# One branch-free stream of 192 slots per expert, with the up projection in unsplit fp32

## The chip, the core and the metric

The kernel runs on one core of a Trainium2 chip. The metric is the device time of one execution in microseconds; a time stands for the median of several executions.

## What is computed

Strided sparse attention (2 batches, 8 heads, 576 tokens, 64 dimensions a head) feeds a dense feed-forward block of 1152 tokens, and that feeds a routed mixture of 8 experts. The change touches the last part only:

```python
logits = x @ w_gate                                   # 1152 tokens, 8 experts
expert_idx = np.argmax(logits, axis=1)
...                                                   # gate_w: softmax probability of the chosen expert
for i in range(N):                                    # first come, first served, capacity 288 an expert
    e = expert_idx[i]
    if counts[e] < capacity:
        disp[e, counts[e]] = x[i]; pos[i] = counts[e]; counts[e] += 1; keep[i] = True
h = np.maximum(np.einsum('ecd,edf->ecf', disp, w1), 0.0)    # 512 -> 1024
y = np.einsum('ecf,efd->ecd', h, w2)                        # 1024 -> 512
out[i] = gate_w[i] * y[expert_idx[i], pos[i]]               # kept tokens, the others are zero
```

All numbers are fp32. Each expert has 2 MB of `w1` and 2 MB of `w2`.

## The kernel before

**Stages.** Attention, then the feed-forward block (`l1`, `l2`, in four groups of 512 hidden columns), with routing work (`r_...` functions) threaded into its last group by `pump`; at the end the experts, one after the other. The order of instructions on each engine is the order in which the code emits them: nothing reorders them, and each engine works through its own queue. DMA loads are issued from SP's queue (weights) and from POOL's (gathers of token rows from `x2d` by `gather`, scatters of results to `out` by `put_out`); an issue that has to wait holds up what stands behind it in that queue.

**Split matmuls.** A value is kept as a high part and a low part in the type fp32r; `mm3` (lines 165 to 168) multiplies in three steps, high by high, high by low and low by high. An fp32r matmul stands in the program as one instruction and in the trace as one weight load and one matmul.

**The expert stage** (from line 1036). Token slots of an expert are three chunks of `ROWS` = 128, 64 and 96. For each expert `e`:

- `prep` (line 922) transposes the gathered rows of chunk 0 and 1 of the next expert (4 matmuls each) and splits them: ACT writes the high part, DVE the low part of `X`.
- `split`/`esplit` (lines 233 to 239) turn each of 8 pieces of 128x1024 raw weights of the next expert into a high part (`whi`, ACT or DVE, line 238) and a low part (`wlo`, DVE or POOL, line 239) and then issue the load of the same piece for the expert after it.
- An expert with at most 128 tokens goes through `narrow`: four `up(i)` of 48 matmuls in all (3 for each of 4 row blocks of `w1`, 256 columns each, tokens as the stationary side), ReLU on ACT, a transpose back (`turn`, line 1083), and `down`, 24 matmuls of 512 columns.
- An expert with more than 128 goes through `wide`: eight `up(i)` of 4 pairs, line 1122 (`whi` against both halves of 192 tokens, 384 columns) and line 1124 (`wlo` against the high half, 192 columns); the two halves of the result are added by ACT and DVE (lines 1127, 1128); ReLU is split again (lines 1136, 1138); `down` is 5 matmuls of 512 columns, three into `y` (tokens 0 to 127) and two into `z` (tokens 128 to 191, both halves stacked).
- Which one is taken is decided on the device. `r_final` writes a flag word, every engine loads it (`get_flags`), and each expert stands under `tc.If` (lines 1226 and 1229; expert 0 under line 1214). Each engine meets these branches in its own queue. A third way, `more`, handles slots beyond 192.

```python
        with tc.If((flags[0] & (3 << 2 * e)) < 1) as small:
            narrow(e, P, y0, fillers(e, False))
        with small.Else():
            with tc.If((flags[0] & (2 << 2 * e)) > 0) as most:
                ...
                wide(e, y0, y1, fillers(e, True), {})
                more(e, y1)
            with most.Else():
                ...
                wide(e, y0, y1, fillers(e, True), {})
        put_out(e, 0, y0)
```

`put_out` (line 1051) scales by the gate and scatters the rows to `out`. For chunk 1 it needs an ACT copy, a DVE add and an ACT scaling. Two scatters in a row wait for each other, since both write `out`.

Of the kernel before, what the change touches and what calls it, by code (L numbers as in the profile page):

```python
# [9 lines left out]
F32 = mybir.dt.float32  # L10
# [8 lines left out]
P = 128  # L19
# [6 lines left out]
N1 = 64  # L26
# [13 lines left out]
W2 = 0  # L40
W3 = 0
LAGW = 3
TT = 3
SPLIT_AT = ((0, 1, 2, 3, 4, 5, 6, 7), (0, 1, 2, 3, 4, 5, 7, 7))
PREP_AT = ((4, 5), (5, 6))
# [3 lines left out]
for _name, _w in (("ident", 128), ("ml", KW), ("ml0", KW), ("ms", 54), ("tri", 128),  # L49
                  ("rev", 8), ("bit", 8), ("tok", 18), ("iota", PW)):  # L50
    _C[_name] = (_off, _w)
    _off += _w
# [4 lines left out]
def constants():  # L57
# [18 lines left out]
    put("bit", np.broadcast_to(4.0 ** np.arange(8), (P, 8)))  # L76
# [12 lines left out]
def tile_kernel(ctx, tc, cap, q, k, v, w_in, w_out, w_gate, w1, w2, consts, out):  # L89
# [125 lines left out]
    SLOTS = ((4, 5, 0, 1), (2, 3, 6, 7))  # L215
    eraw = {}

    def eload(e, h):
        if e >= E:
            return  # L220
        j, r = divmod(h, 2)
        if e == 0 or (e == 1 and h < 4):
            eraw[e, h] = rawp.tile([P, 2, 512], F32, tag="raw", name="raw")
        elif e == 1:
            eraw[e, h] = rawq.tile([P, 2, 512], F32, name=f"raw{h}")
        else:
            eraw[e, h] = eraw[1, h]
        if j < 2:
            src = w1[e][:, 512 * j:512 * j + 512].rearrange("(k p) f -> p k f", p=P)
        else:  # L230
            src = w2[e][512 * (j - 2):512 * (j - 1), :].rearrange("(c p) n -> p c n", p=P)
        nc.sync.dma_start(out=eraw[e, h], in_=src[:, 2 * r:2 * r + 2])

    def esplit(e, h, hi, lo):
        raw = eraw[e, h]
        j, r = divmod(h, 2)
        slot, k = SLOTS[e % 2][j], slice(2 * r, 2 * r + 2)
        (nc.scalar.copy if hi == "A" else nc.vector.tensor_copy)(whi[slot][:, k], raw)  # L238
        (nc.vector if lo == "D" else nc.gpsimd).tensor_sub(wlo[slot][:, k], raw, whi[slot][:, k])  # L239
# [373 lines left out]
    for s in range(2, 6):  # L613
        alloc_w(wpb, s)

# [184 lines left out]
    def r_final():  # L800
# [4 lines left out]
        f = rp.tile([1, 2, E], F32, name="flag", bufs=1)  # L805
        for j in range(2):
# [234 lines left out]
    for i in (6, 7):  # L1041
        alloc_w(wpc, i)
# [225 lines left out]
```

## Time and profile before

| | |
|---|---|
| median of 3 runs | 510.21 us |
| lowest, highest | 506.58 us, 512.13 us |
| span of the profiled execution, first to last instruction | 507.0 us |
| TensorE (PE) busy, share of that span | 87% |
| mean granted TensorE clock | 0.920 |

The span is that of one execution; the device time of an execution also holds what lies around its first and last instruction, which the profile does not show. In the profile PE is TensorE's matmuls, PEld its weight loads, DVE VectorE, ACT ScalarE, POOL GpSimd, SP SyncE. "Issue" as a releaser means that the engine waited for nothing that the profile shows.

### The profile page before, as it was taken

How to read it: one execution, taken by the hardware profiler on the slowest of the kernel's cores; microseconds unless marked ns; L12 is line 12 of the kernel's file. 1: busy time of each engine (PE TensorE's matmuls, PEld its weight loads, DVE VectorE, ACT ScalarE, POOL GpSimd, SP SyncE). 2: the span in 40 equal slices, each digit the busy share in tenths (PEclk: the TensorE clock that was granted, in tenths of full speed). 3: DMA queues.
4: the chain of work that ended last, by engine and by line, in shares of the span. 5: the costliest groups of instructions: out<-in, count | busy, mean ns of one | idle time of the engine just before them, and what ended most of it. 6: DMA issues, size and time to landing. Idle time of an engine off the chain costs nothing.

```text
span 507.0 us, 8500 instructions
## 1 busy us (share of the span) xinstructions
PE 443.6 (87%) x2959; PEld 377.6 (74%) x2959; DVE 345.1 (68%) x782; ACT 235.8 (47%) x587; POOL 198.8 (39%) x180
## 2 busy tenths in 40 slices
PE   8899998999998999999999998798547949498885
PEld 4577677899897899989998788686537748286774
DVE  3569899357788837885445877948684929559571
ACT  4568677245543433444443435355334425244631
POOL 0225433013232311336552154639664426263550
PEclk9969699999998999999999997989796969879989
DMA  7899727023343311344441126735863636535300
GB/s 158 177 233 230 202 85 244 10 53 113 124 126 95 114 41 62 105 125 123 127 146 43 63 75 209 229 127 204 294 224 130 222 116 197 180 113 194 108 25 22
DMA packets 52194, 69.33 MB, mean 137 GB/s; under 512 B 19608, under 2 KB 29080, under 8 KB 52124
## 3 DMA queue, kind: packets, MB, share of 16 engines
q1 hardware_dynamic: 50268, 63.18, 42.1%
q0 software_dynamic: 1856, 5.26, 2.9%
q8 instruction: 38, 0.62, 0.6%
q14 instruction: 32, 0.26, 0.2%
HBM read 61.60 MB, written 7.34 MB: 136 GB/s over the span
## 4 chain that ended last, share of the span: by engine, by line
PE 49%; DVE 23%; issue 13%; ACT 6%; DMA 6%; POOL 1%; POOLq 0%; DVEq 0%; ACTq 0%; another core or an unknown queue 0%
DVE wlo L239 5%; PE acc L166 5%; DVE wsb L194 4%; PE acc L167 4%; DMA out_dram<-y,idx_o 4%; PE h L166 4%; PE h L168 4%; PE acc L168 4%; PE h L167 4%; PE u L1122 4%; DVE g L261 2%; PE acc L406 2%; DVE gl L269 2%; ACT gh L268 2%; PE acc L466 2%
## 5 line engine op out<-in xcount | busy, mean ns | idle before, releaser
L239 POOL TENSOR_TENSOR wlo<-raw,whi 128x1024 fp32r<-128x1024 f32 x36 | 88.9, 2479 | 58.7 <-ACT whi L238 40.0
L203 POOL TENSOR_TENSOR wlo<-w,whi 128x512 fp32r<-128x512 f32 x32 | 44.3, 1385 | 117.6 <-DVE gl L269 79.5
L1122 PE MATMUL u<-X,whi 128*128 128x384 f32 x128 | 49.2, 437 | 24.5 <-issue 24.5
L239 DVE TENSOR_TENSOR wlo<-raw,whi 128x1024 fp32r<-128x1024 f32 x28 | 64.6, 2307 | 5.1 <-ACT whi L238 4.9
L166 PE MATMUL acc<-whi,gh 128*128 128x512 f32 x144 | 59.0, 410 | 2.8 <-DVE x L290 2.8
L166 PE MATMUL h<-xhi,whi 128*128 128x384 f32 x176 | 60.1, 341 | 0.0
L168 PE MATMUL h<-xhi,wlo 128*128 128x384 f32 x176 | 59.5, 338 | 0.0
L167 PE MATMUL h<-xlo,whi 128*128 128x384 f32 x176 | 59.5, 338 | 0.0
L167 PE MATMUL acc<-wlo,gh 128*128 128x512 f32 x144 | 58.1, 403 | 0.0
L168 PE MATMUL acc<-whi,gl 128*128 128x512 f32 x144 | 57.3, 398 | 0.0
L238 ACT CAST whi<-raw 128x1024 fp32r<-128x1024 f32 x50 | 52.4, 1054 | 0.0
L268 ACT CAST gh<-g 128x384 fp32r<-128x384 f32 x48 | 24.6, 513 | 59.1 <-DVE g L261 59.1
L1122 PEld LDWEIGHTS u<-X,whi 128*128 128x128 f32 x128 | 29.9, 234 | 26.6 <-issue 25.8
L261 DVE TENSOR_TENSOR g<-h,g 128x384 f32<-128x384 f32 x44 | 24.3, 553 | 34.8 <-ACT g L260 34.8
L269 DVE TENSOR_TENSOR gl<-g,gh 128x384 fp32r<-128x384 f32 x48 | 28.1, 585 | 25.6 <-ACT gh L268 25.5
L260 ACT ACTIVATE g<-h 128x384 f32<-128x384 f32 x44 | 21.5, 489 | 48.5 <-PE h L168 48.3
L194 DVE SCALAR_TENSOR_TENSOR wsb<-raw,wsb 128x512 uint32<-128x512 uint32 x32 | 39.2, 1226 | 1.0
L421 ACT ACTIVATE pr<-sc,st 128x54 f32<-128x54 f32 (+1 forms) x84 | 28.8, 345 | 19.8 <-DVE st L418 19.8
L1124 PE MATMUL u<-X,wlo 128*128 128x192 f32 x128 | 36.4, 285 | 0.0
L166 PEld LDWEIGHTS h<-xhi,whi 128*128 128x128 f32 x176 | 33.1, 188 | 2.1
L167 PEld LDWEIGHTS h<-xlo,whi 128*128 128x128 f32 x176 | 33.1, 188 | 1.9
L166 PEld LDWEIGHTS acc<-whi,gh 128*128 128x128 f32 x144 | 27.5, 191 | 8.2 <-ACT w L191 3.6
(246 smaller groups left out, 1036.8 us busy)
## 6 DMA issues: line engine op xcount, KB each, us to landing
raw<-in_moe_w_dram SPq DMA_DIRECT2D x64, 512.0 KB
raw<-in_moe_w_in_dram SPq DMA_DIRECT2D x16, 512.0 KB
raw<-in_moe_w_out_dram SPq DMA_DIRECT2D x16, 512.0 KB
out_dram<-zw SPq DMA_DIRECT2D x1, 2304.0 KB
x2d<-x SPq DMA_DIRECT2D x2, 768.0 KB
vl<-in_v_dram SPq DMA_DIRECT2D x4, 288.0 KB
kr<-in_k_dram SPq DMA_DIRECT2D x4, 288.0 KB
qr<-in_q_dram SPq DMA_DIRECT2D x4, 288.0 KB
```

Source lines behind the costliest of these rows:

```text
L166: nc.tensor.matmul(o, lhsT=ah, rhs=bh, start=first, stop=False)
L167: nc.tensor.matmul(o, lhsT=ah, rhs=bl, start=False, stop=False)
L168: nc.tensor.matmul(o, lhsT=al, rhs=bh, start=False, stop=last)
L194: nc.vector.scalar_tensor_tensor(out=u, in0=top, scalar=0x80000000, in1=u, op0=ALU.bitwise_and, op1=ALU.bitwise_or)
L203: nc.gpsimd.tensor_sub(wlo[slot][:, k], t, whi[slot][:, k])
L238: (nc.scalar.copy if hi == "A" else nc.vector.tensor_copy)(whi[slot][:, k], raw)
L239: (nc.vector if lo == "D" else nc.gpsimd).tensor_sub(wlo[slot][:, k], raw, whi[slot][:, k])
L261: nc.vector.tensor_mul(a, h, a)
L268: nc.scalar.copy(gh, a)
L269: nc.vector.tensor_sub(gl, a, gh)
L1122: nc.tensor.matmul(hp[:, 0:2 * NW], lhsT=whi[j][:, kk, o:o + P], rhs=x[:, kk].rearrange("p a n -> p (a n)"), start=kk == 0, stop=False)
L1124: nc.tensor.matmul(hp[:, 0:NW], lhsT=wlo[j][:, kk, o:o + P], rhs=x[:, kk, 0], start=False, stop=kk == KC - 1)
```

## The change

The routing up to the flag stays. In the expert stage:

- `w1` is no longer split: its pieces are loaded straight into whole fp32 tiles `w1b` (three of them, in turn), those of experts 0 and 1 during the feed-forward block. `X` is one fp32 tile.
- Every expert takes 192 slots: `up` is 4 matmuls in plain fp32 of 192 columns each, `relu` reads the result from PSUM and splits it, `down` is that of `wide`.
- The eight experts are one sequence of 64 steps, without a branch; `down` runs 3 steps behind `up`, across the seam between experts.
- `w2` is split as before, 4 pieces an expert, two experts ahead of need in loading, high part on ACT, low part on DVE (expert 0: on POOL, in the feed-forward block).
- Slots beyond 192 are handled under a single `tc.If` at the end, which loads and splits all weights again; its flag is set if any expert has more than 192 tokens.
- `put_out` for chunk 1 takes one ACT and one DVE instruction instead of three, and both result tiles have two buffers.

```diff
+    def w1load(e, j):
+        if e < E:
+            for r in range(2):
+                nc.sync.dma_start(out=w1b[e % 3][:, 2 * r:2 * r + 2, 512 * j:512 * j + 512],
+                                  in_=w1[e][256 * r:256 * r + 256, 512 * j:512 * j + 512]
+                                  .rearrange("(k p) f -> p k f", p=P))
...
+    def split(e, h, ahead=2):
...
+        nc.scalar.copy(whi[slot][:, k], raw)
+        (nc.vector if e else nc.gpsimd).tensor_sub(wlo[slot][:, k], raw, whi[slot][:, k])
+        w2load(e + ahead, h)
...
-        xh, xl = (X[e % 2][:, :, i, o:o + n] for i in range(2))
-        nc.scalar.copy(xh, src)
-        nc.vector.tensor_sub(xl, src, xh)
+        nc.vector.tensor_copy(X[e % 2][:, :, o:o + n], src)
...
-            nc.scalar.copy(y[:n], yp[N1:2 * N1])
-            nc.vector.tensor_add(y[:n], yp[:n], y[:n])
-            nc.scalar.mul(y[:n], y[:n], g)
+            nc.scalar.activation(out=y[:n], in_=yp[N1:2 * N1], func=AF.Copy, scale=g)
+            nc.vector.scalar_tensor_tensor(out=y[:n], in0=yp[:n], scalar=g, in1=y[:n], op0=ALU.mult, op1=ALU.add)
...
-    def narrow(e, n, yp, fill):
...
-    def wide(e, y0, y1, fill, tt, part=(0, 8)):
...
+    def up(e, i, n=NW):
+        hp = psum("u")
+        for kk in range(KC):
+            nc.tensor.matmul(hp[:, 0:n], lhsT=w1b[e % 3][:, kk, P * i:P * i + P], rhs=X[e % 2][:, kk, 0:n],
+                             start=kk == 0, stop=kk == KC - 1)
+        return hp
+
+    def relu(hp, parts, n=NW):
+        t = ep.tile([P, 2 * NW], F32R, tag="ht", name="ht", bufs=LAG + 1)
+        nc.scalar.activation(out=t[:, 0:n], in_=hp[:, 0:n], func=AF.Relu)
+        for o, c, m in parts:
+            nc.vector.scalar_tensor_tensor(out=t[:, o:o + m], in0=hp[:, c:c + m], scalar=0.0, in1=t[:, c:c + m],
+                                           op0=ALU.max, op1=ALU.subtract)
+        return t
...
     for e in range(E):
...
+        fill(e, 3 if e == 0 else 0, (gather, e + 2, 0))
+        fill(e, 4 if e == 0 else 1, (gather, e + 2, 1))
+        for h in range(4):
+            fill(e, SPLIT_AT[h], (split, e + 1, h))
+        fill(e, 5, (prep, e + 1, 0))
+        fill(e, 6, (prep, e + 1, 1))
+        for j in range(2):
+            fill(e, 3 + 4 * j, (w1load, e + 3, j))
+    fill(3, 0, (get_flags,))
...
+    for s in range(8 * E + LAG):
+        e, i = divmod(s, 8)
+        if s < 8 * E:
+            hp = up(e, i)
+        d, c = divmod(s - LAG, 8)
+        if s >= LAG:
+            if c == 0:
+                ys[d] = psum("y"), psum("z")
+            down(d, c, ht.pop((d, c)), *ys[d])
+        for f, *args in fills.pop((e, i), []):
+            f(*args)
+        if s < 8 * E:
+            ht[e, i] = relu(hp, PARTS)
+        if s >= LAG and c == 7:
+            y0, y1 = ys.pop(d)
+            put_out(d, 1, y1)
+            put_out(d, 0, y0)
...
+    with tc.If(flags[0] > 0):
...
```

**Where the instructions stand, PE.** On PE, at the seam between expert 0 and expert 1. Before, expert 0's last `down` ends at two branches, behind which expert 1's `narrow` begins (`h` is its PSUM tile, `X_3345` the tokens):

```order
L1149 MATMUL z<-whi_97,kept_3699 128x512
L1150 MATMUL z<-wlo_98,kept_3699 64x512
L1150 MATMUL z<-wlo_98,ht 64x512
L1152 MATMUL z<-whi_97,ht 128x512
L166 MATMUL y<-whi_97,ht 128x512
L167 MATMUL y<-wlo_98,ht 128x512
L168 MATMUL y<-whi_97,ht 128x512
L1214 UNCONDITIONAL_BRANCH
L1226 REGISTER_ALU
L1226 COMPARE_AND_BRANCH
L166 MATMUL h<-whi_1515,X_3345 128x256
L167 MATMUL h<-wlo_1516,X_3345 128x256
```

Now, the last `up` of expert 0 (`X_3334`, `w1b_1519`), a `down` of expert 0, and the first `up` of expert 1 (`X_3335`, `w1b_1520`):

```order
L1055 MATMUL u<-X_3334,w1b_1519 128x192 x4
L161 MATMUL y<-whi_97,ht 128x512
L162 MATMUL y<-wlo_98,ht 128x512
L163 MATMUL y<-whi_97,ht 128x512
L1074 MATMUL z<-whi_97,ht 128x512
L1075 MATMUL z<-wlo_98,ht 64x512
L1055 MATMUL u<-X_3335,w1b_1520 128x192 x4
```

The branches are gone from PE's queue, the ups of expert 1 stand before the last three downs of expert 0, and an `up` is 4 instructions where `wide` had 8.

**DVE.** On DVE, two steps of a wide expert before: the sum of the two halves (`hs`), the low part of a weight piece, the two low parts of the ReLU, the next sum, and a high part of a weight piece:

```order
L1128 TENSOR_TENSOR hs<-u,hs 128x192
L239 TENSOR_TENSOR wlo_1522<-raw,whi_1521 128x1024
L1138 SCALAR_TENSOR_TENSOR ht<-hs,ht 128x64
L1138 SCALAR_TENSOR_TENSOR ht<-hs,ht 128x128
L1128 TENSOR_TENSOR hs<-u,hs 128x192
L238 CAST whi_95<-raw_3684 128x1024
```

Now, two steps in the stream, the second with the copy of the next expert's tokens:

```order
L236 TENSOR_TENSOR wlo_98<-raw_3675,whi_97 128x1024
L1063 SCALAR_TENSOR_TENSOR ht<-u,ht 128x64
L1063 SCALAR_TENSOR_TENSOR ht<-u,ht 128x128
L932 COPY X_3334<-m 128x4x128
L1063 SCALAR_TENSOR_TENSOR ht<-u,ht 128x64
L1063 SCALAR_TENSOR_TENSOR ht<-u,ht 128x128
```

The sums and the high parts of weights are gone from DVE; the low parts of the ReLU now read PSUM (`u`) directly.

## Rows read from the trace of the kernel before

**Rows 1.** Page: granted TensorE clock in 40 slices, tenths of full speed.
```profile
PEclk9969699999998999999999997989796969879989
```

**Rows 2.** Stretches: length, busy us PE, PEld, DVE, ACT, POOL; clock, DMA share, GB/s.
```profile
0.00:307.30 307.30, 295.12 (x2136) 249.62 (x2137) 211.65 (x591) 150.15 (x419) 98.88 (x122) 0.95 0.43 119
307.30:501.30 194.00, 148.46 (x830) 127.93 (x826) 133.43 (x192) 84.97 (x168) 98.90 (x58) 0.87 0.51 168
336.70:352.20 15.50, 13.44 (x89) 11.58 (x87) 10.14 (x11) 11.19 (x20) 11.04 (x7) 1.00 0.47 167
352.20:383.10 30.90, 15.26 (x89) 13.30 (x89) 21.85 (x15) 10.21 (x17) 19.70 (x10) 0.81 0.79 268
...
501.30:507.00 5.70, 0.00 (x1) 0.00 (x0) 0.00 (x0) 0.69 (x1) 0.99 (x1) 0.80 0.11 45
```

**Rows 3.** PE's waits in the expert stage: us in total, times, longest us.
```profile
PE u L1122 <- issue: 24.5, 4, 9.4
PE m L1083 <- DVE wlo L239: 7.0, 2, 5.9
PE z L1152 <- DVE ht L1138: 7.0, 3, 2.4
PE m L931 <- DVE tt L1086: 3.5, 2, 3.3
PE h L166 <- issue: 2.1, 1, 2.1
PE m L804 <- DVE idx L778: 1.4, 1, 1.4
```

**Rows 4.** Line 1229, TensorE's sequencer: duration ns min/median/max, first and last start us.
```profile
L1229 PEldq COMPARE_BRANCH  x3: 4934/5615/6585, 377.9 to 437.9; - x3
```

**Rows 5.** Groups of PE, shapes apart: busy us, mean ns of one, idle before.
```profile
L1122 PE MATMUL u<-X,whi 128*128 128x384 f32 x128 | 49.2, 437 | 24.5 <-issue 24.5
...
L406 PE MATMUL acc<-kt,qs 64*64 64x96 f32 x144 | 9.1, 261 | 1.0 <-ACT qs L379 0.5 <-DVE qs L379 0.5
```

**Rows 6.** Timeline of PE in expert 0: start us, length us.
```profile
315.00 0.36 PE L1122 MATMUL u<-X,whi 128*128 128x384 f32 x1
315.20 0.25 PE L1124 MATMUL u<-X,wlo 128*128 128x192 f32 x1
315.29 0.37 PE L1122 MATMUL u<-X,whi 128*128 128x384 f32 x1
...
315.58 0.42 PE L166 MATMUL y<-whi,ht 128*128 128x512 f32 x1
...
316.76 0.31 PE L786 MATMUL m<-R,mt 128*128 128x24 bf16 x6
```

**Rows 7.** Plain fp32 matmuls: timeline of a run, and ns of one (min/median/max).
```profile
15.88 0.58 PE L406 MATMUL acc<-kt,qs 64*64 64x96 f32 x10
...
L406 PE MATMUL acc<-kt,qs x10: 242/243/243, 15.9 to 16.2; 64*64 64x96 f32 x10
...
296.22 0.83 PE L652 MATMUL h<-wg,xt 128*128 128x24 f32 x6
...
L652 PE MATMUL h<-wg,xt x6: 269/270/270, 296.2 to 296.8; 128*128 128x24 f32 x6
L652 PEld LDWEIGHTS h<-wg,xt x5: 192/192/192, 296.3 to 296.7; 128*128 128x128 f32 x5
```

**Rows 8.** DVE's weight subtraction (line 239) and ReLU remainder (line 1138), ns min/median/max.
```profile
L239 DVE TENSOR_TENSOR wlo<-raw,whi x28: 1207/1636/8244, 314.1 to 490.4; 128x1024 fp32r<-128x1024 f32 x28
...
L1138 DVE SCALAR_TENSOR_TENSOR ht<-hs,ht x58: 208/277/2411, 311.4 to 468.3; 128x64 fp32r<-128x64 f32 x29, 128x128 fp32r<-128x128 f32 x29
```

**Rows 9.** The scatter, line 1063: the last one, and landing times of all.
```profile
502.30 0.99 POOL L1063 DMA_INDIRECT out_dram<-y,idx_o  x1 [11.05 <-ACT y L1062]
...
DMA to landing us min/median/max: 2.2/3.2/6.9
```

**Rows 10.** Busy us and granted clock in a stretch of the attention stage.
```profile
54.20:64.40 10.20, 10.12 (x78) 7.85 (x77) 8.32 (x37) 7.07 (x29) 5.53 (x7) 0.50 0.64 190
```

More of the change, by code (lines that the diff above doesn't have):

```diff
@@ L39 @@
 WHOLE = 6
[L40 to L45, printed above, removed]
+LAG = 3
+SPLIT_AT = (0, 2, 4, 6)
 _C = {}
@@ L911, in tile_kernel @@
     xg2 = eg.tile([P, DM], F32, name="xg2")
-    X = [eg.tile([P, KC, 2, NW], F32R, name=f"X{i}") for i in range(2)]
+    X = [eg.tile([P, KC, NW], F32, name=f"X{i}") for i in range(2)]
     def xg_of(e, ch):
@@ L1166, in fillers @@
-    def fillers(e, wide):
-        steps = [[] for _ in range(9)]
-        for c in range(2):
-            steps[PREP_AT[wide][c]].append((prep, e + 1, c))
-        for h in range(8):
-            steps[SPLIT_AT[wide][h]].append((split, e + 1, h))
-        steps[0].append((gather, e + 2, 0))
-        steps[1].append((gather, e + 2, 1))
-        return filler(steps)
-    def filler(steps):
-        def fill():
-            for f, *args in (steps.pop(0) if steps else []):
-                f(*args)
-        return fill
@@ L1183, in tile_kernel @@
-    for h in range(4, 8):
-        eload(1, h)
+    def up(e, i, n=NW):
[11 more added lines that the diff above has]
+        return t
@@ new lines, in down @@
+    def down(e, i, t, y0, y1):
+        j, c = 2 * (e % 2) + i // 4, i % 4
+        for y in ((y1, y0) if i == 7 else (y0, y1)):
+            if y is y0:
+                mm3(y0, t[:, 0:P], t[:, 2 * P:3 * P], whi[j][:, c], wlo[j][:, c], i == 0, i == 7)
+            else:
+                if i < 7:
+                    nc.tensor.matmul(y1, lhsT=t[:, P:2 * P], rhs=whi[j][:, c], start=i == 0, stop=False)
+                nc.tensor.matmul(y1[:N1], lhsT=t[:, P:NW], rhs=wlo[j][:, c], start=False, stop=False)
+                if i == 7:
+                    nc.tensor.matmul(y1, lhsT=t[:, P:2 * P], rhs=whi[j][:, c], start=False, stop=True)
@@ new lines, in tile_kernel @@
+    assert not fills, fills
+    with tc.If(flags[0] > 0):
+        n = ROWS[2]
+        for e in range(E):
+            gather(e, 2)
+            w1b[e % 3] = w1b[0]
+            for j in range(2):
+                w1load(e, j)
+            for h in range(4):
+                w2raw[e, h] = w2raw[1, h]
+                nc.sync.dma_start(out=w2raw[e, h],
+                                  in_=w2[e][256 * h:256 * h + 256, :].rearrange("(c p) n -> p c n", p=P))
+                split(e, h, E)
+            prep(e, 2)
+            y2 = psum("y")
+            for i in range(8):
+                t = relu(up(e, i, n), ((n, 0, n),), n)
+                j, c = 2 * (e % 2) + i // 4, i % 4
+                mm3(y2[:n], t[:, 0:n], t[:, n:2 * n], whi[j][:, c], wlo[j][:, c], i == 0, i == 7)
+            put_out(e, 2, y2)
```

225 lines of the change are left out of this document (46 added, 179 removed).

## The prediction

> **What bounds the kernel now.** I read the page first, then the stretches, then PE's waits in the last one, then single rows. PE is busy for 87% of the span, but the clock row shows where that is not useful: it is at 9 for most slices of the feed-forward block and falls to 6 to 8 in the last third [rows 1]. The stretches say why. Up to 307.3 us PE is busy 295 of 307 us; there it is the bound, and the change hardly touches it. From 307.3 to 501.3, the expert stage, PE is busy 148.5 of 194.0 us [rows 2]. So 45.5 us are idle, and the six waits that PE lists there add up to the same: 24.5 + 7.0 + 7.0 + 3.5 + 2.1 + 1.4 [rows 3]. The largest, 24.5 + 2.1 us "issue" in front of the first matmul of an expert, is the branch: TensorE's sequencer spends 4.9 to 6.6 us in each of the three compare-and-branches of line 1229 [rows 4]. Three of the others (7.0, 3.5 and 7.0) are waits for DVE, the longest of them (5.9) for its weight subtraction, which takes 1.2 us at best and up to 8.2 [rows 8]; POOL does the other half of these subtractions at the same time.
>
> The second loss is the clock. What the stage's work costs at full clock: a wide expert has 32 pairs of up matmuls at 315.29 - 315.00 = 0.29 us, 9.3 us, and eight downs at 316.76 - 315.58 = 1.18 us, 9.4 us [rows 6]; with some 0.8 us of token transposes that is 19.5. A narrow one is the stretch 336.7 to 352.2, at clock 1.00: 13.4 us [rows 2]. Line 1122 has 128 records, 32 an expert, so four experts are wide and four narrow [rows 5]. 4 x 19.5 + 4 x 13.4 = 132 us; the other 17 of the 148.5 are work at half clock, behind the idle gaps.
>
> So the stage is 132 us of work, 17 of half clock and 45 of idleness. The change adds work and takes away idleness.
>
> **The change, part by part.**
>
> *The up projection.* Plain fp32 matmuls stand in the attention stage. Line 406 issues 72 of 96 columns (4 head pairs, 9 blocks, 2 halves) and has 144 records [rows 5]: two records each. Ten records in two parallel streams take 0.58 us, one 0.243, so five in a row are 4 steps of (0.58 - 0.243)/4 = 0.084 us [rows 7]. For 192 columns I take twice that, 0.168 us a record, 0.336 a matmul. The bounds: 0.16 if part of the 0.084 is fixed; 0.20 from the split matmul of 384 columns, the wait for the next weights included [315.00 to 315.20, rows 6]. An up is 8 records: 1.34 us (1.28 to 1.60). Thus a wide expert's ups go from 9.3 to 10.8 us: the unsplit form is no cheaper on PE; what it saves is the splitting on ACT, DVE and POOL.
>
> *192 slots for all.* Every expert has eight downs of 1.18 us [rows 6]. One step is 1.34 + 1.18 = 2.52 us, 64 steps 161.5 us. Token transposes for seven experts: four of 128 columns and four of 64, by the 0.084 us for 96 columns 0.7 us and a little more for their start, 0.8 each, 5.6 us. A narrow expert thus goes from 13.4 to 21.0 us, a wide one from 19.5 to 21.0; the stage's work from 132 to 167.
>
> *The branches.* Gone from PE's queue until the last matmul: 26.6 us of idleness and most of the 17 us of half clock go with them. What is late next in their place is PE's own work, if everything else keeps up.
>
> *The other engines.* Per expert of 21 us DVE has 4 subtractions, 16 ReLU remainders, 2 copies of tokens and 1 sum. At the undisturbed 1.2 us and some 0.3 us, and under 1 us for each of the rest, that is 4.8 + 4.8 + 2 = 12 us; with subtractions at the median 1.6 us 13 us [rows 8]. Both are hidden behind 21 us of PE, and POOL, which slowed DVE, has only gathers and scatters left. ReLU remainders are queued behind a subtraction on DVE, so a result can be 1.2 to 2 us late; downs stand three steps, 7.6 us, behind, which covers it. ACT has 4 copies, 8 ReLUs and 2 scalings and is less loaded than DVE (85 against 133 us busy now) [rows 2]. If this cover failed, each late subtraction would cost PE up to its own 1.2 us, 4 an expert.
>
> *Loads.* Of 33.5 MB of expert weights 8.4 lie ready at 307 us (experts 0 and 1). The other 25.2 MB, with some 5 MB of gathered and scattered rows, are wanted by the time expert 7 starts, 147 us later: 205 GB/s. The trace has 268 GB/s over 31 us [rows 2], so I cost this at nothing. SP's queue holds loads that wait for a buffer, but nothing is wanted sooner than an expert after its issue. The 4 MB loaded early share the feed-forward stretch, which runs at 119 GB/s [rows 2]; PE does not wait there.
>
> *Expert 0.* The routing matmuls and the wait of 1.4 us for DVE [rows 3] stay; the clock is still at half for the first 3 us. Together I put 4 us on it (2 to 8: the first three steps are now ups alone).
>
> *The end.* Now one scatter follows the last matmul: 501.3 to 507.0, 5.7 us [rows 2, 9]. After the change expert 7 has two, and the second waits for the first to land, 3.2 us in the median [rows 9], of which some 0.7 overlap the last three downs into `y`. The end becomes 8.2 us (7 to 12). The one branch left stands behind PE's last matmul; at 4.9 to 6.6 us [rows 4] it lies beside the scatters.
>
> *Sum.* Start 307.0 (the split of expert 0's first tokens loses a DVE pass). 161.5 + 5.6 + 4 = 171.1; last matmul at 478.1. I add 5 us, 0.6 an expert, for short waits that no row prices (0 to 15): 483. The end: 483 + 8.2 = 491.2 us of span against 507.0. The median of the runs shown is 510.2, 3.2 over that span, and I carry the 3.2 along: **494.5 us**, 15.7 less than the median.
>
> **A rule that speaks against it.** The weights of back-to-back plain fp32 matmuls on the full array: six records of line 652 have a weight load of 0.192 us and a matmul of 0.27 each, and still follow each other at (0.83 - 0.27)/5 = 0.112 us [rows 7]. Loads run under matmuls. The Trainium skill ("TensorE: Matmul & The Clock Gate", Part 3, "What overlaps and what doesn't") says that a weight load overlaps running matmuls only if it goes to another row group. By that rule the 64 records of an expert would each pay their load; the trace does not agree, with 0.112 us where load and matmul in a row would be more than 0.192. It is the third rival below.
>
> **The rivals.**
>
> 1. *Supply or DVE falls behind, about no change.* Place: SP's queue from expert 2 on, or the subtraction in front of a ReLU. For it: the mean rate of the stage is 168 GB/s [rows 2], and if loads ran no faster, 30 MB would take 179 us, 32 beyond the 147; at 190 GB/s 11 beyond. Against it: 168 is what was asked for, and the trace has 268. With 10 to 15 us of such waits the time is 505 to 510.
>
> 2. *Half clock in the fp32 stream, slower.* From 54.2 to 64.4 us PE is busy 10.12 of 10.2 us, mostly with plain fp32 matmuls and transposes, and the clock stays at 1.2 GHz [rows 10]. If ups in plain fp32 do not hold the clock at 2.4, a step takes twice 2.52 us: 161 us more if it is always so, 80 if half the time, around 575. It decides from 15.7/161 = 10% of the stage on. Against it: those matmuls use a quarter of the array each, while the ups fill it and nearly half of each step is the same fp32r work that holds the clock through the feed-forward block [rows 1].
>
> 3. *Weight loads not hidden, slower.* Each of 64 x 8 records pays 0.112 us more [rows 7]: 57 us, 552. Against it stands the row that gives that 0.112.
>
> 4. *The change does not do what it says:* an expert has over 192 tokens, the last branch is taken, and all weights are loaded again, 33.5 MB at 268 GB/s, 125 us more. Against it: no matmul of the third way is among the groups now; 128 records in line 1122 are four wide experts and no more.
>
> **How the numbers follow.** Forecast 0.77, rival 1 0.11, rival 2 0.07, rival 3 0.04, rival 4 0.01. A measurement of this kernel can tell about 1% from no change, so "faster" is below 505.1 us, "slower" above 515.3. Of the forecast's share nearly all lies below 505 (its own range, from a record of 0.16 to one of 0.18 us and waits of 0 to 10: 483 to 506); rival 1 is half within 1%, the rest on both sides. Faster 0.79, within 1% 0.09, slower 0.12. The low end, 483, has records of 0.16 us and no waits: 64 x 0.06 = 4 us and 5 us less, and 2 from the end. The high end, 512, takes in records of 0.20 us (64 x 8 x 0.032 = 16 us more) and all but the worst of rival 1; rivals 2 to 4 are left out.
>
> **What would show each step right or wrong.** Right: records of line 1055 at 0.16 to 0.17 us; steps of about 2.5 us; PE idle under 10 us between the first up and the last matmul; clock 1.00 from expert 1 on; subtractions near 1.2 us; two scatters behind the last matmul. Wrong: records at 0.28 us (rival 3), clock at 0.5 in dense steps (rival 2), waits of `whi` for DMA or of PE for DVE that add up to over 15 us (rival 1), any instruction of the last branch's body (rival 4). The prediction falls if the last matmul is later than about 495 us.

## The result, and the profile after

The changed kernel takes 483.1 us (median of 4 runs, 482.0 to 488.5) beside 508.4 us of the kernel before (4 runs, 502.7 to 512.1): a ratio of 0.956, 95% interval 0.948 to 0.964. The forecast was 494.5 us, faster; the result lies 0.1 us inside the low edge of its range of 483 to 512. The direction was right, and the time was still 11 us better than forecast. The profiled execution is one of the runs behind a median and can be the slowest of them (in one case below 499.3 us beside a median of 491.3).

The clock row of the page, which answers to [rows 1]:

```profile
PEclk9987999999999999999999999799999999999996
```

The dips to 6 to 8 in the last third are gone. The 7 that is left stands at 301 to 313 us, where expert 0 begins, and the 6 is the end, where no matmul runs.

Stretches of the kernel after, columns as in [rows 2]: the expert stage from its first up to the last matmul, expert 1 alone, and the end.

```profile
303.50:470.30 166.80, 166.75 (x926) 146.20 (x923) 75.44 (x195) 57.51 (x107) 29.81 (x33) 0.99 0.53 173
323.10:343.70 20.60, 20.60 (x113) 18.13 (x112) 9.86 (x23) 7.72 (x15) 3.86 (x4) 1.00 0.76 257
470.30:481.50 11.20, 0.00 (x0) 0.00 (x0) 0.74 (x1) 0.69 (x1) 1.90 (x2) 0.62 0.07 26
```

The stage has shrunk from 194.0 us to 166.8, and PE is busy in all but 0.05 us of it. The list of PE's waits in the stage, six rows before [rows 3], has no row now. The clock is 1.00 in expert 1 and 0.99 on the whole. DVE's work in the stage has fallen from 133.4 to 75.4 us, POOL's from 98.9 to 29.8.

The first up starts 3.8 us earlier than before, at 303.5 instead of 307.3. That need not be the change's doing: the code up to there is nearly the same, and in the profiled executions shown here the first up starts anywhere from 298.7 us (granted clock up to there 0.99) to 314.2 (0.92). So below, stages are compared from their first up to PE's last matmul, and not only whole times.

PE's plain fp32 matmuls and its last branch; DVE's weight subtraction and ReLU remainder (ns of one, min/median/max), which answer to [rows 4, 7, 8]:

```profile
L1055 PE MATMUL u<-X,w1b x512: 323/326/667, 303.5 to 465.3; 128*128 128x192 f32 x171
...
L1132 PEldq COMPARE_BRANCH  x1: 3771/3771/3771, 466.6 to 466.6; - x1
```

```profile
L236 DVE TENSOR_TENSOR wlo<-raw,whi x28: 1214/1224/1227, 305.1 to 442.7; 128x1024 fp32r<-128x1024 f32 x28
...
L1063 DVE SCALAR_TENSOR_TENSOR ht<-u,ht x128: 214/252/283, 306.6 to 466.2; 128x64 fp32r<-128x64 f32 x64, 128x128 fp32r<-128x128 f32 x64
```

The subtraction that took up to 8.2 us before never takes more than 1.23 now, and the remainder's longest is 0.28 us instead of 2.41.

One step of the stream, on PE:

```profile
330.43 1.46 PE L1055 MATMUL u<-X,w1b 128*128 128x192 f32 x8
331.60 0.53 PE L161 MATMUL y<-whi,ht 128*128 128x512 f32 x1
331.96 0.39 PE L162 MATMUL y<-wlo,ht 128*128 128x512 f32 x1
332.19 0.39 PE L163 MATMUL y<-whi,ht 128*128 128x512 f32 x1
332.42 0.40 PE L1074 MATMUL z<-whi,ht 128*128 128x512 f32 x1
332.65 0.39 PE L1075 MATMUL z<-wlo,ht 128*64 128x512 f32 x1
332.88 0.32 PE L1055 MATMUL u<-X,w1b 128*128 128x192 f32 x1
```

A step is 332.88 - 330.43 = 2.45 us. The eight records follow each other at (1.46 - 0.326)/7 = 0.162 us. The first matmul of the down sits 0.36 us ahead of the next one, the others 0.23. That is no delay: its own start is recorded only 0.04 us behind that of the eighth record (330.43 + 7 x 0.162 = 331.56), so the two distances together are 0.40, as 0.162 + 0.23 would be, and 8 x 0.162 + 5 x 0.23 = 2.45 is the whole step.

The end, on POOL:

```profile
471.33 0.91 POOL L1048 DMA_INDIRECT out_dram<-y,idx_o  x1 [11.94 <-DVEq L1132]
474.22 0.98 POOL L1048 DMA_INDIRECT out_dram<-y,idx_o  x1 [1.98 <-ACTq L1132]
```

Two scatters follow the last matmul, as forecast, the second 2.9 us after the first.

So the numbers say "faster", and PE is the bound. What they don't say is which part of the change did it: the branches that are gone, to which the prediction gave the whole gain, or the splitting that is gone, which it booked as work on other engines that frees no time on PE by itself. Both are gone at once here. The experiments take them apart.

### The profile page after: what moved, and what is told of

Read it like the earlier page. It is cut to its first block, busy times and chain, and to the rows that moved or that the text cites. A ratio compares the mean times of both kernels' runs of the same rounds, so it can differ in the third digit from the quotient of the medians.

```text
span 481.5 us, 8430 instructions
## 1 busy us (share of the span) xinstructions
PE 455.1 (95%) x3053; PEld 390.3 (81%) x3055; DVE 285.5 (59%) x785; ACT 203.8 (42%) x521; POOL 120.5 (25%) x152
## 5 line engine op out<-in xcount | busy, mean ns | idle before, releaser
L1055 PE MATMUL u<-X,w1b 128*128 128x192 f32 x512 | 95.7, 331 | 0.0
L1055 PEld LDWEIGHTS u<-X,w1b 128*128 128x128 f32 x512 | 86.1, 192 | 6.3
L1061 ACT ACTIVATE ht<-u 128x192 fp32r<-128x192 f32 x64 | 21.2, 331 | 105.0 <-PE u L1055 65.2
L162 PE MATMUL acc<-wlo,gh 128*128 128x512 f32 x144 | 56.7, 394 | 0.0
L1063 DVE SCALAR_TENSOR_TENSOR ht<-u,ht 128x64 fp32r<-128x64 f32 (+1 forms) x128 | 26.9, 252 | 46.7 <-ACT ht L1061 46.7
L1048 POOL DMA_INDIRECT out_dram<-y,idx_o x16 | 15.5, 966 | 124.1 <-DVE y L1045 81.7
L267 DVE TENSOR_TENSOR gl<-g,gh 128x384 fp32r<-128x384 f32 x48 | 26.7, 557 | 25.7 <-ACT gh L266 25.5
L236 DVE TENSOR_TENSOR wlo<-raw,whi 128x1024 fp32r<-128x1024 f32 x28 | 34.2, 1222 | 9.2 <-ACT whi L235 9.2
```

The source lines that it names most:

```text
L162: nc.tensor.matmul(o, lhsT=ah, rhs=bl, start=False, stop=False)
L236: (nc.vector if e else nc.gpsimd).tensor_sub(wlo[slot][:, k], raw, whi[slot][:, k])
L267: nc.vector.tensor_sub(gl, a, gh)
L1055: nc.tensor.matmul(hp[:, 0:n], lhsT=w1b[e % 3][:, kk, P * i:P * i + P], rhs=X[e % 2][:, kk, 0:n], start=kk == 0, stop=kk == KC - 1)
L1063: nc.vector.scalar_tensor_tensor(out=t[:, o:o + m], in0=hp[:, c:c + m], scalar=0.0, in1=t[:, c:c + m], op0=ALU.max, op1=ALU.subtract)
```

## Experiments

Times are medians, the ratio in brackets is that to the kernel before on the same chip, with its 95% interval. "Stage" is the length from the first up to PE's last matmul in the profiled execution (before: 194, after: 166.7).

### The branches alone

**Before without branches, all experts wide.** Of the kernel before only the expert loop is changed:

```diff
-        with tc.If((flags[0] & (3 << 2 * e)) < 1) as small:
-            narrow(e, P, y0, fillers(e, False))
-        with small.Else():
...
+        y0, y1 = psum("y"), psum("z")
+        wide(e, y0, y1, fill, {})
+        put_out(e, 0, y0)
```

> The kernel before, with every expert through the wide path in straight code: no branch, 192 slots, up projection still split; slots beyond 192 are left out (no expert here has them). Theory A (the gain came from PE's idle gaps at the branches and the half clock behind them, and the split up is no dearer on PE): 8 experts of 19.5 us, 4 us for expert 0 and some 1.9 us of waiting for DVE at each seam give a stage of about 173 us, a time of 485 to 495. Rival B (splitting w1 on ACT, DVE and POOL is what held the stage up, and unsplit fp32 is what made it fast): experts of 24 us or more, a time of 503 or more.

Measured: 523.1 us (1.042, 1.033 to 1.051). The four wide experts of the kernel before, then the stage and one expert of this one:

```profile
307.30:336.70 29.40, 24.90 (x150) 21.18 (x147) 23.99 (x52) 11.99 (x26) 14.68 (x13) 0.84 0.65 215
383.10:413.40 30.30, 22.56 (x112) 19.26 (x113) 19.88 (x33) 13.03 (x27) 12.62 (x7) 0.84 0.49 158
413.40:444.80 31.40, 22.66 (x113) 19.50 (x113) 19.88 (x33) 13.04 (x27) 13.63 (x8) 0.83 0.51 161
444.80:469.50 24.70, 22.26 (x112) 19.30 (x113) 19.22 (x32) 11.54 (x25) 12.71 (x7) 0.89 0.49 164
```

```profile
307.40:512.20 204.80, 172.67 (x925) 141.72 (x921) 154.91 (x276) 95.10 (x207) 99.94 (x60) 0.95 0.46 158
387.50:413.80 26.30, 21.95 (x114) 17.66 (x112) 20.55 (x33) 12.56 (x27) 14.37 (x8) 0.95 0.51 180
```

Without branches the same four experts take 27.0, 26.3, 26.5 and 25.9 us, 105.7 together instead of 115.8. So the branches did cost 10 us there, where the prediction's prices (19.5 for a wide expert, 4 more for expert 0) would have made it 34. The four experts that were narrow took 194.0 - 115.8 = 78.2 us together (15.5 the first of them [rows 2]) and take 99.1 now that they are wide, and the stage is 10.8 us longer. PE's waits in it:

```profile
PE z L1152 <- DVE ht L1138: 18.9, 7, 2.9
PE y L168 <- DVE ht L1138: 12.4, 14, 3.4
```

Now PE waits for DVE instead, 31.3 us. That is the part of the prediction's sentence that carried the load: "What is late next in their place is PE's own work, if everything else keeps up." With `w1` split, everything else does not keep up.

**The new stream, with `w1` still split.** The order of the kernel after (64 steps, downs three steps behind, across the seams, the shorter `put_out`), with the pieces of before and without the last branch; the cut is against the kernel after:

```diff
-            nc.tensor.matmul(hp[:, 0:n], lhsT=w1b[e % 3][:, kk, P * i:P * i + P], rhs=X[e % 2][:, kk, 0:n],
-                             start=kk == 0, stop=kk == KC - 1)
+            nc.tensor.matmul(hp[:, 0:2 * NW], lhsT=whi[j][:, kk, o:o + P],
+                             rhs=x[:, kk].rearrange("p a n -> p (a n)"), start=kk == 0, stop=False)
+            nc.tensor.matmul(hp[:, 0:NW], lhsT=wlo[j][:, kk, o:o + P], rhs=x[:, kk, 0],
+                             start=False, stop=kk == KC - 1)
...
+        nc.scalar.copy(s, hp[:, NW:2 * NW])
+        nc.vector.tensor_add(s, hp[:, 0:NW], s)
```

> The new stream of 64 steps with down three steps behind up, but the up projection split as before (384 + 192 columns) on the buffers of the kernel before; slots beyond 192 are left out. Theory A: an up of four pairs of 0.286 us in place of eight records of 0.1625 is 0.16 us a step less, 64 steps 10 us; stage about 157 us, time 470 to 477, so faster than the changed kernel. Rival B (the additional splitting collides on DVE and POOL and PE waits): 483 or more, with PE waits for DVE or POOL in the stage.

Measured: 520.0 us (1.036, 1.027 to 1.044). The stage, then what ACT waits for in it:

```profile
301.40:504.60 203.20, 173.38 (x924) 146.98 (x921) 135.33 (x275) 93.92 (x200) 102.92 (x60) 0.91 0.47 159
```

```profile
ACT ht L1214 <- DVE hs L1212: 76.5, 64, 3.6
```

203 us: the order of the stream is worth 1.6 us at most by itself (the stages of the kernel after and of the last run below, nearly the same code, differ by 1.1 us). The unsplit up is worth 203.2 - 166.7 = 36.5 us of the stage, although its own matmuls on PE are dearer (8 x 0.162 = 1.30 us against 4 x 0.29 = 1.16 [rows 6]). The kernel after also loads weights further ahead, but that is not it: in the split stream no engine's list of waits in the stage has a load of weights in it. The remaining runs ask why. On DVE there are 17 us of work in an expert of 26; it isn't full. But ACT waits for DVE in every one of the 64 steps.

### What the splitting costs

Three causes were thinkable: DVE is held up beside POOL's subtractions; DVE and ACT have too much to do; ACT and DVE hand the result to and fro (copy, sum, ReLU, remainder) and each hand-over waits behind what stands in the queue. A stretch of that stream shows the first and the third:

```profile
375.35 0.43 DVE L1216 SCALAR_TENSOR_TENSOR ht<-hs,ht 128x64 fp32r<-128x64 f32 x2 [0.43 <-ACT ht L1214]
...
376.33 2.41 POOL L240 TENSOR_TENSOR wlo<-raw,whi 128x1024 fp32r<-128x1024 f32 x1 [1.60 <-ACT whi L239]
376.42 0.32 ACT L1211 COPY hs<-u 128x192 f32<-128x192 f32 x1
...
376.89 0.34 DVE L1212 TENSOR_TENSOR hs<-u,hs 128x192 f32<-128x192 f32 x1
...
377.27 0.36 ACT L1214 ACTIVATE ht<-hs 128x192 fp32r<-128x192 f32 x1 [0.53 <-DVE hs L1212]
...
377.67 1.35 DVE L1216 SCALAR_TENSOR_TENSOR ht<-hs,ht 128x64 fp32r<-128x64 f32 x2 [0.43 <-ACT ht L1214]
```

The two remainders take 0.43 us when POOL is idle and 1.35 when POOL subtracts: the first of them lasts until POOL's subtraction ends, at 376.33 + 2.41 = 378.74, and the second has its usual 0.28 us behind that (377.67 + 1.35 - 0.28 = 378.74). Of the 22 remainders that start during a POOL subtraction in this stage, 21 end 0.08 to 0.09 us behind it. And the chain ACT, DVE, ACT, DVE is there in full.

**All subtractions on DVE.** This run and the next three change the split stream:

```diff
-    MODE = (("A", "P"), ("A", "D"), ("A", "P"), ("A", "D"), ("D", "P"), ("A", "D"), ("A", "P"), ("D", "D"))
+    MODE = (("A", "D"), ("A", "D"), ("A", "D"), ("A", "D"), ("D", "D"), ("A", "D"), ("A", "D"), ("D", "D"))
```

> The stream with w1 still split (520 us) is taken, and the half of the weight subtractions that POOL does (4 an expert, 2.4 us each) goes to DVE, where an undisturbed one takes 1.22 us. Theory 'collision': a ReLU remainder on DVE that starts while POOL subtracts lasts until POOL is done (1.1 to 1.5 us for 0.22); without POOL's work the remainders are back at 0.22, DVE has some 18 us of work per expert instead of 17, and PE's waits shrink: 22 to 25 us per expert, 500 to 512 us in all. Theory 'volume' (DVE and ACT simply have too much to do): 4 x 1.22 us more on the engine that PE waits for, 26 to 29 us per expert, 520 to 540.

Measured: 516.9 us (1.019, 1.009 to 1.028), stage 202.5.

```profile
L1216 DVE SCALAR_TENSOR_TENSOR ht<-hs,ht x128: 224/254/289, 310.0 to 505.4; 128x64 fp32r<-128x64 f32 x64, 128x128 fp32r<-128x128 f32 x64
```

The longest remainder is 0.29 us; in the stream before it was 1.92. The collision is gone, and the stage stays as long. Neither theory's time came: collision wanted 500 to 512, volume 520 to 540. Taking the hold-ups away and putting 4 x 1.22 us of subtractions an expert into DVE's queue came out even.

**POOL's half left out.**

```diff
+        if e < 2 or lo == "D":
             (nc.vector if lo == "D" else nc.gpsimd).tensor_sub(wlo[slot][:, k], raw, whi[slot][:, k])
```

> The stream with w1 still split (520 us), but from expert 2 on the half of the low parts of w1 and w2 that POOL makes is left out (those experts use low parts of earlier weights). DVE and ACT keep all their instructions. Theory 'collision': 21 to 22.5 us per expert from expert 1 on instead of 26, about 490 to 497 us. Theory 'volume': DVE's and ACT's lists are unchanged, so 25 us or more per expert, 512 to 520.

Measured: 495.1 us (0.978, 0.969 to 0.987), stage 179.2; 22.4 us per expert. With DVE's list unchanged, POOL's share of the splitting is worth 24 us of the stage. That fits "collision" and not "volume". It goes only two thirds of the way to 166.7, and the run above says that moving the work to DVE doesn't earn it. DVE is busy for only 111.8 of the 179.2 us here, 62%.

**Without the sum of the halves.** All splitting stays; ReLU and remainder read the up's result in PSUM directly:

```diff
-        s = ep.tile([P, 256], F32, tag="hh", name="hs")[:, 0:NW]
-        nc.scalar.copy(s, hp[:, NW:2 * NW])
-        nc.vector.tensor_add(s, hp[:, 0:NW], s)
+        s = hp[:, 0:NW]
```

> The stream with w1 still split (520 us, 26 us per expert), without the sum of the two halves of an up's result: 8 ACT copies of 0.32 us and 8 DVE additions of 0.35 us an expert go, and with them two of the four hand-overs between ACT and DVE in a step. Left out is the product of w1's high part with the tokens' low part. All subtractions stay, POOL's too. Theory 'hand-overs' (ACT and DVE wait for each other in turn, 3.2 us a step): 20 to 22 us per expert, 480 to 492 us. Theory 'collision' (DVE held up beside POOL's subtractions): those stay, 23.5 us or more per expert, 500 to 515.

Measured: 479.4 us (0.946, 0.938 to 0.953), stage 169.8, as fast as the kernel after. The stage, DVE's weight subtractions, high parts and remainders, then DVE's and ACT's waits in experts 1 to 7:

```profile
306.80:476.60 169.80, 159.96 (x925) 136.43 (x921) 128.74 (x212) 75.94 (x137) 110.07 (x68) 0.98 0.56 190
```

```profile
L240 DVE TENSOR_TENSOR wlo<-raw,whi 128x1024 fp32r<-128x1024 f32 x28 | 50.8, 1815 | 3.6 <-ACT whi L239 2.9
L239 DVE CAST whi<-raw 128x1024 fp32r<-128x1024 f32 x14 | 38.3, 2738 | 0.0
...
L1214 DVE SCALAR_TENSOR_TENSOR ht<-u,ht x128: 208/250/284, 308.8 to 472.5; 128x64 fp32r<-128x64 f32 x64, 128x128 fp32r<-128x128 f32 x64
```

```profile
DVE ht L1214 <- ACT ht L1212: 14.1, 10, 1.9
```

```profile
ACT ht L1212 <- issue: 36.1, 21, 7.8
ACT X L935 <- PE m L932: 21.1, 12, 2.6
ACT ht L1212 <- PE u L1205: 15.7, 8, 2.0
```

DVE is busy for 128.7 of 169.8 us, 76% (67% in the stream with the sum), and POOL for 110 us, and PE still runs nearly through. So it is not the volume. Nor is it DVE's hold-ups as such: its subtractions take 50.8 us here where they took 36.4 in the split stream, and its high parts of weights 38.3 where they took 9.6, so beside POOL it loses more than the remainders lost there (38.5 us for 64 that take 0.22 undisturbed), and the stage is 33 us shorter all the same. ACT no longer waits for DVE anywhere in its list; the result goes one way, ACT to DVE to PE, and the three steps between up and down swallow what is late. One part of this edit can't be told apart: the remainder's first operand is now in PSUM, and beside POOL it isn't held up any more (below). But the run with all subtractions on DVE had no hold-up either and stayed at 202.5, so the hand-overs, and what stands ahead of them in DVE's queue, are needed to explain the 26 us an expert.

**A second bank for `z`.** PE's listed wait in the split stream is for `z` (24.9 us in 7 waits).

```diff
-    banks(u="h0 h1 a0", m="m0 a3", y="f0 a1", z="a2")
+    banks(u="h0 h1", m="m0 a3", y="f0 a1", z="a2 a0")
```

> The stream with w1 still split (520 us), with a second PSUM bank for z, taken from u (three to two). PE's listed wait in that stream is for z, 24.9 us in 7 times. Theory 'bank' (it is z's single bank that costs the time): the wait goes, 22 to 23 us per expert, 488 to 500 us. Theory 'DVE and ACT are late': the same time is waited for elsewhere, at u or at ht, 25 to 27 us per expert, 512 to 528.

Measured: 517.3 us (1.022, 1.016 to 1.028), stage 201.7.

```profile
PE u L1203 <- DVE hs L1212: 29.0, 16, 3.6
```

The wait moved from `z` to `u` and grew to 29.0 us. The row that is listed names the place where the delay surfaces and not its cause: DVE is late, and whichever bank runs out first shows it.

**The kernel after, with half of its subtractions on POOL.**

```diff
-        (nc.vector if e else nc.gpsimd).tensor_sub(wlo[slot][:, k], raw, whi[slot][:, k])
+        (nc.vector if e and h % 2 else nc.gpsimd).tensor_sub(wlo[slot][:, k], raw, whi[slot][:, k])
```

> The kernel after (483 us), with two of the four w2 subtractions of an expert moved from DVE to POOL. DVE has 2.4 us less to do per expert. Theory 'collision': remainders that start beside POOL's subtraction take 1 to 2.4 us instead of 0.22, though the three steps between up and down (7.4 us) may still hide this: 483 to 490 us. Theory 'volume': remainders stay at 0.22 us and DVE's busy time falls by 17 us; 483 us.

Measured: 483.1 us (0.952, 0.943 to 0.961), stage 167.4, PE busy in 167.35 us of it.

```profile
L1063 DVE SCALAR_TENSOR_TENSOR ht<-u,ht x128: 207/250/282, 308.3 to 468.1; 128x64 fp32r<-128x64 f32 x64, 128x128 fp32r<-128x128 f32 x64
```

```profile
L236 DVE TENSOR_TENSOR wlo<-raw,whi x14: 1212/1226/4074, 312.0 to 444.5; 128x1024 fp32r<-128x1024 f32 x14
```

The remainders were not held up, against what "collision" said; DVE's own subtractions were, up to 4.07 us for 1.22. It costs nothing here: where the result goes one way, a DVE instruction 3 us late is covered by the three steps of 2.45 us.

### What a branch costs

In the kernel after, seven branches whose bodies never run are put back, one in each expert from 1 to 7, on the flag that every engine loads. The three runs differ only in the number of matmuls that the jump passes over (`warm(1, ...)`, `warm(128, ...)`, `warm(512, ...)`):

```diff
-    fill(3, 0, (get_flags,))
+    fill(0, 5, (get_flags,))
+
+    def branch():
+        with tc.If(flags[0] > 0):
+            warm(128, "m")
+
+    for e in range(1, E):
+        fill(e, 4, (branch,))
```

> The changed kernel with seven untaken branches in the middle of experts 1 to 7, one matmul in the body of each. Theory A (a branch costs by how much code it jumps over): TensorE's sequencer needs well under 1 us for each, PE's queue covers it, time within 2 us of the changed kernel (483 to 486). Rival C (any branch stalls PE's sequencer for 3 to 6 us): 7 x about 2 us beyond what the queue covers and some half clock, 495 to 520.

> The same with 128 matmuls in each untaken body. Theory A: 3.3 to 6.6 us for each of the seven compare-and-branches on TensorE's sequencer as in the kernel before, of which PE's queue covers up to 3: gaps of 1 to 4 us, 7 to 28 us in all, half clock behind the longer ones: 490 to 520. If the jump's distance does not matter it is the same as with one matmul in the body.

> The kernel after with seven branches that are not taken, as in the two runs before, but each jumps over 512 matmuls instead of 128 or 1. Theory 'distance' (a branch whose target lies far away in the program has to have its instructions fetched): each takes 3 to 6 us on PE's sequencer, as in the kernel before and as the last branch of the kernel after (3.8 us), PE idles for most of that and some half clock follows: 7 x 3 to 5 us more, 505 to 525 us. Rival (before's branches were long because PE's sequencer came to them with nothing queued or waited for the flag, not for their length): 0.2 to 0.4 us each, 485 to 490 us.

Measured: 489.6 us with 1 matmul (0.975, 0.959 to 0.992), 487.6 with 128 (0.971, 0.955 to 0.987), 491.3 with 512 (0.967, 0.957 to 0.976); stages 168.3, 168.4 and 171.7. By the medians that is 4.4 to 8.1 us more than the kernel after, with only two runs for each of the first two; the stages hold 1.6, 1.7 and 5.0 us of it, and where the rest lies is not shown. The branch on TensorE's sequencer (ns min/median/max), with 1, 128 and 512 matmuls to jump over:

```profile
L1111 PEldq COMPARE_BRANCH  x7: 202/202/238, 332.5 to 458.8; - x7
```

```profile
L1111 PEldq COMPARE_BRANCH  x7: 313/313/367, 330.8 to 457.1; - x7
```

```profile
L1111 PEldq COMPARE_BRANCH  x7: 3382/3947/4306, 342.9 to 471.0; - x7
```

With 1 matmul the branch costs 0.2 us, as theory A had it, though the time is above its 483 to 486; with 128 it was expected to cost 3.3 to 6.6 us and costs 0.3. With 512 it meets what was expected of a far jump on the sequencer, 3 to 6 us, and misses the time of 505 to 525. So what takes 3.4 to 4.3 us is the distance of the jump. That is the class of [rows 4] (4.9 to 6.6) and of line 1132 (3.8). The Trainium skill ("Advanced Engine Details and Errata", "Control Flow Timing" and "ISA Cache") gives about 108 ns for a compare-and-branch, and an instruction cache in lines of 256 instructions. The short branches here take two to three times that figure, 0.20 and 0.31 us. That the price at 512 matmuls has to do with the cache fits the rows, but no run shows it.

But even seven far jumps lengthen the stage by only 5.0 us, 0.7 each, as far as single executions can tell. Around the first of them, which lasts from 342.9 to 347.1:

```profile
346.25 0.39 PE L1075 MATMUL z<-wlo,ht 128*64 128x512 f32 x1
347.28 1.54 PE L1055 MATMUL u<-X,w1b 128*128 128x192 f32 x8 [0.64 <-PEq L1111]
```

PE had 3.7 us of matmuls in hand when its sequencer came to the branch, worked through them, and idled 0.64 us. In the kernel before, in front of the branch that lasts from 407.5 to 413.2:

```profile
406.77 0.50 PE L1152 MATMUL z<-whi,ht 128*128 128x512 f32 x1 [2.30 <-DVE ht L1138]
...
407.57 0.40 PE L168 MATMUL y<-whi,ht 128*128 128x512 f32 x1
413.43 0.66 PE L1122 MATMUL u<-X,whi 128*128 128x384 f32 x1 [5.46 <-issue]
```

There the matmul ahead of the branch waited for DVE until 406.8, so the sequencer came to the branch with only 0.4 us of work in hand, and nearly the whole jump, 5.5 us, was idle. Here the losses of the kernel before are one chain: DVE late, no lead, far jump in full, and the clock at 0.50 (1.2 GHz) from 409.2 to 419.4 us. That holds for two of the four waits of "issue 24.5" (5.5 and 6.5 us, both behind a wait for DVE). In the other two PE had work in hand and the jumps were longer than it: 2.8 us ahead of a jump of 5.8, and 3.4 us ahead of three in a row (4.0, 3.3 and 4.9), which gave the wait of 9.4.

### The padding, and the end

**One short branch an expert.** The flag of before (more than 128 tokens) skips what only tokens 128 to 191 need on PE; the matmuls into `z` are put together behind the last down into `y`, `ht` keeps 12 buffers, and the weight pieces are split at other steps:

```diff
+    def down1(e, ts, y1):
+        with tc.If((flags[0] & (3 << 2 * e)) > 0) if e else nullcontext():
+            for i in range(8):
...
+            if c == 7:
+                down1(d, [ht.pop((d, i)) for i in range(8)], ys[d][1])
```

> The kernel after (483 us), with the 16 matmuls of an expert into z (tokens 128 to 191) put together behind its last down into y, under one branch an expert that skips them where it has at most 128 tokens; expert 0 always does them. The flag word is the one of the kernel before, the last branch stays. Theory 'a short jump is cheap': four experts do without 16 matmuls of some 0.23 us, 3.6 us each, 14.5 in all; seven branches at 0.3 to 0.7 us give 2 to 5 back: 470 to 475 us. Rival (what made branches dear before, PE waiting for another engine at the branch, comes back here, 2 to 4 us each): 480 to 500 us.

Measured: 473.7 us (0.933, 0.925 to 0.941; after: 0.948 to 0.964), faster than both kernels. The stage, a period that holds expert 0's block, and one in which expert 1's is skipped:

```profile
309.40:462.50 153.10, 152.06 (x864) 134.34 (x860) 73.48 (x196) 56.35 (x107) 35.96 (x40) 1.00 0.55 194
326.10:346.80 20.70, 20.70 (x114) 18.16 (x113) 9.57 (x24) 7.67 (x14) 4.89 (x4) 1.00 0.72 265
346.80:364.30 17.50, 17.20 (x98) 15.45 (x97) 9.45 (x25) 7.59 (x14) 4.50 (x4) 1.00 0.76 264
```

```profile
L1076 PEldq COMPARE_BRANCH  x10: 76/176/372, 349.5 to 460.7; - x10
```

A skipped block gives 3.2 us, the branch costs 0.1 to 0.4 on the sequencer, and the stage is 13.7 us shorter. (Ten records for seven branches: the three bodies that run have a second one at their end.) Branches as such are no enemy of the stream.

**Without the last branch.**

```diff
-    with tc.If(flags[0] > 0):
-        n = ROWS[2]
-        for e in range(E):
...
```

> The kernel after without the branch at its end; slots beyond 192, of which these inputs have none, are left out, so that part of the computation is missing. Theory 'the end waits for the branch's join': POOL's last two instructions (0.8 and 2.7 us) no longer follow the landing of the last scatter in a row, and the end behind PE's last matmul falls from 11.2 to 8 to 9 us, 480 to 481 us in all. Rival (the landing of the second scatter alone sets the end): 11 us stay, 483 us.

Measured: 482.0 us (0.946, 0.938 to 0.955); by the medians no different from the kernel after. The end in the profile does differ:

```profile
464.30:472.90 8.60, 0.00 (x0) 0.00 (x0) 0.74 (x1) 0.69 (x2) 1.90 (x2) 0.69 0.08 28
```

```profile
468.12 0.98 POOL L1048 DMA_INDIRECT out_dram<-y,idx_o  x1 [1.85 <-issue]
```

8.6 us instead of 11.2. The second scatter is issued 3.8 us behind the last matmul in this kernel and 3.9 in the kernel after; from there it is 4.8 us to the end here and 7.3 there. So the join behind the last branch is worth 2.5 us at the end, which the profile resolves and the medians, whose runs spread over 10 us, don't. The other traces bear it out: the end is 11.0 to 11.2 us in the kernel after and the four runs on it that keep that branch and the same order (with 1, 128 and 512 matmuls to jump over, and with subtractions on POOL), and 8.6 in the five runs on the split stream, which has no last branch.

## Why the prediction was right, and where it was not

**The way and the bound: right.** "Right" was to show as records at 0.16 to 0.17 us, steps of about 2.5, PE idle under 10 us, clock 1.00 from expert 1, subtractions near 1.2 us and two scatters at the end. They are 0.162, 2.45, 0.05, 1.00, 1.22 and two. Rival 1 (supply) did not come: the stage moved 173 GB/s, expert 1 257, and PE waited for nothing. Rival 2 (half clock in the fp32 stream) did not: 0.99. Rival 3 would have shown records at 0.28 us; they stand at 0.162, so loads run under matmuls with a full array too, as the earlier row of 0.112 had it. No instruction of rival 4's body ran.

**The sum, term by term.**

| term | predicted | measured | difference |
|---|---|---|---|
| first up | 307.0 | 303.5 | -3.5, varies from execution to execution |
| 64 steps | 64 x 2.524 = 161.5 | 64 x 2.45 = 156.8 | -4.7 |
| transposes, 7 experts | 5.6 | 7 x (20.65 - 8 x 2.45) = 7.4 | +1.8 |
| expert 0, first and last steps | 4 | 166.7 - 156.8 - 7.4 = 2.5 | -1.5 |
| short waits | 5 | 0 | -5 |
| the end | 8.2 | 11.2 | +3.0 |
| outside the span | 3.2 | 483.3 - 481.5 = 1.8 | -1.4 |

Together -11.3: 494.5 becomes 483.2, the profiled execution's 483.3. (20.65: experts 1 and 7 start at 323.09 and 447.04, six periods of 20.66.)

Most sizes have a reason. The step: 0.168 a record was twice that of a 96-column record, 0.162 it is, so the lower bound ("0.16 if part of the 0.084 is fixed") was the nearer one, worth 3.1 of the 4.7 us; the rest is the down, 5 x 0.23 = 1.15 us where 1.18 was taken. The waits: 5 us were added for what no row prices, and nothing came. The end: that the one branch left "lies beside the scatters" is true of PE, whose 3.8 us end with the last matmul, and false of the join behind it, which adds 2.5 us; without it the end is 8.6, where 8.2 was forecast. The 3.2 us were the distance of one span to a median of runs that spread over 5.5 us, and not what lies around a span. The first up varies by far more than 0.1 us from execution to execution, so it is luck that the result lies just inside the range and not just outside.

**The step that failed** is the booking of the gain. The prediction wrote: "Gone from PE's queue until the last matmul: 26.6 us of idleness and most of the 17 us of half clock go with them", and of the unsplit up, "what it saves is the splitting on ACT, DVE and POOL", with no time on PE to its credit. It thereby gave the branches' removal the whole gain. With the branches removed and all experts wide the kernel takes 523 us, with the new order as well 520, both slower than before; the branches' removal is worth 10 us in the four wide experts. Put back into the kernel after, seven far jumps cost 5.0 us. The gain comes with the unsplit up: 36.5 us of the stage between the split stream and the kernel after. The prediction's price is reached only if everything else keeps up, a condition that it stated, gave to rival 1, and priced for the kernel after. There it held. So the time was right for a reason that the prediction had: it added up PE's work in the kernel after, and that sum does not depend on which part of the change ended the idleness.

**The reading that misled** is "issue 24.5 us" beside branches of 4.9 to 6.6 us [rows 3, 4]. Both are right, and the branch was indeed what PE waited for. But a far jump of 4 us costs PE 0.7 us where PE has 3.7 us of work in hand. That it had 0.4 in two of the four waits was DVE's lateness, listed two rows below with 7.0 us, where it looked three and a half times smaller than the branch. And a list of waits names what ends last: with the branches gone, the waits for DVE's `ht` grew from 7.0 us to 31.3.

**The cover, as said:** DVE's 12 to 13 us per expert were forecast, 75.4/8 = 9.4 measured; "downs stand three steps, 7.6 us, behind, which covers it" held even with subtractions stretched to 4.1 us. **The padding, as said:** a narrow expert was to go from 13.4 to 21.0 us, and went to 20.65; 3.2 us of that can be had back for a branch of 0.1 to 0.4.

Still open is how the 36.5 us divide between hand-overs and POOL's hold-ups: leaving out the sum removes both for the remainder, leaving out POOL's work removes the second alone, and moving it to DVE puts its time into the queue that the hand-overs wait behind. A stream with copy, sum and ReLU on one engine was not tried.

## What to carry to other kernels

Work on an engine that is not full still sets the pace when a result goes to and fro between two in-order queues: count the hand-overs of a step and what may stand ahead of each, not only the busy time. A change that saves the bound engine nothing and shortens that chain can be worth more than the idle time that the wait list shows first. And a branch is priced by its distance and by the work in hand when it is reached: on the sequencer a short one costs 0.1 to 0.4 us and a far one 3.4 to 4.3, of which 0.7 us were left where PE had 3.7 us of work in hand; nearly all of it is idle time where PE has just waited for another engine.

## What the runs showed of the hardware that was not expected

- A branch that skips its body takes 0.20, 0.31 or 3.95 us (medians) on TensorE's sequencer for 1, 128 and 512 matmuls in that body, and seven of the last kind lengthen the stage by 5 us in all.
- A DVE instruction beside a POOL subtraction waits for that to end or not at all, by its operands. The remainder with both inputs in SBUF (`hs`, `ht`) took up to 1.92 us for 0.22; with one input in PSUM (`u`, `ht`) it stayed at 0.28 or less in all 51 cases in which it started beside the same POOL instruction (33 in the run without the sum, 18 in the one with subtractions on POOL); DVE's subtraction of two SBUF tiles took up to 4.07 for 1.22. One SBUF input is not enough to be spared: the high part of a weight piece (`whi`, read from SBUF and written to it) took up to 9.75 us for 0.68 in the run without the sum, across four POOL subtractions in a row. The Trainium skill ("SBUF — State Buffer", "SBUF: two separate sides") says that DVE and GpSimd take one pair of ports exclusively and for a whole instruction, and names two SBUF inputs among the cases; the rows with two SBUF inputs agree.
- Plain fp32 matmuls of 128x128 by 192 columns follow each other at 0.162 us a record, two records a matmul, and the change to fp32r matmuls of 512 columns (0.23 us each) and back costs nothing that the trace shows: 8 x 0.162 + 5 x 0.23 is the step of 2.45 us.
